# mLSTM cell and multiplicative FFN on one core: one pair of last products and its sums moved up two steps, y's transposes put ahead of k's and q's

## Chip, cores and metric

The kernel runs on one NeuronCore of one Trainium2 chip. The metric is the device time of one execution in microseconds (us); less is better. The engines are named as the profile names them: PE is TensorE (matmuls and transposes), PEld its weight loads, DVE is VectorE, ACT is ScalarE, POOL is GpSimd, SP is SyncE, which here only issues DMAs.

## The reference

Two blocks follow each other. The first is an mLSTM cell over 4 batches, 8 heads, 768 time steps and a head size of 40; the second is a feed-forward network on 3072 tokens of 320 features:

```python
for t in range(S):                       # 768 steps; q, k, v, gates are inputs
    m_new  = max(f_gate + m, i_gate)
    f_stab = exp(f_gate + m - m_new); i_stab = exp(i_gate - m_new)
    C = f_stab * C + i_stab * outer(v_t, k_t)
    n = f_stab * n + i_stab * k_t
    y_t = sigmoid(o_gate) * (C @ q_t) / max(abs(n . q_t), 1)
x = y as (3072, 320)
a = x @ w1; b = x @ w2                   # 320 x 1024 each
out = ((a * b) @ w3) @ w_out             # w3 1024 x 1024, w_out 1024 x 320
```

## The kernel before, in words

**Units and steps.** The tokens are cut into 24 units of 128 tokens of one batch (six stretches of time by four batches; `NU = 24`, `NT2 = 6`, `B = 4`). One Python loop over `s` writes 32 steps (0 to 31). In step `s` the cell forms the scores and the state of unit `s` and the outputs of unit `s-1` (`quarter_work`), and `y` of unit `s-2` is brought into the turned form `x` that the network needs. Everything is fp32. The program order of each engine is the order in which this loop writes its instructions; matmuls and transposes are chained by hand (`in_order`, used by `mm` at L92 and `transpose` at L95), so PE does exactly what is written, in that order.

**The first ten steps.** For units below 10, k and q are turned by PE: `turn(n)` writes four transposes of k and four of q into two PSUM tiles (`pt`), and ACT copies each out (`kT`, `qT`, L322). For units below 15, `y` is turned by PE too: `twice(n)` lets POOL copy 64 columns of `y` to its end (L467), `x_trans(n)` writes three transposes (`px`; the third one reads the copied columns) and one ACT copy into `xT` (L477). At the end of step `s`, `turn(s+1)` comes first and `x_trans(s-2)` after it. At these steps PSUM has four tiles for this work (`mps`, a ring of four). A matmul into a tile waits until the tile's last reader is done.

**The network.** Tokens go through in six groups of four units. For groups 0 to 2, `up` forms blocks of `a` and `b` (PSUM `pa`, `pb`; 128x256 moving), `up_rest` adds the last 64 of the 320 inputs, ACT scales `a` (`a_sb`, L626) and DVE multiplies into `ab` (L627). An `up` of half a group reads the `x` of two units: step 6 is the first to read units 2 and 3, step 8 the first to read units 4 and 5. w3 and w_out are multiplied together once (`wp`, then `w3o`), so that the last product is `ab @ w3o`; `ffn_out` does it for 14 blocks of 128 tokens.

**Seven products.** Groups 3 to 5 use a form with seven products of quarters for eight, at the price of sums. `up_by_seven` (one of 12 blocks in each of steps 19 to 30) is written in parts: `shared` (PSUM `p15`, `p67`, shown as `p`), `single` and `left` (PSUM `pa`, `pb`), `product`. DVE adds PSUM into the kept parts in `wo` (L674, L672), POOL finishes them (L699) and multiplies into `ab` (L717). `token_sums` are DVE's sums of `x` for it (L654, written to a tile named `w3T`), made after DVE has turned a late unit's `y` (`x_turn`, L463), which comes back from a trip through DRAM.

`out_by_seven` does the last product for five pairs of 128-token blocks: (3,1) in step 27, (4,0) in step 29 and three in step 31. Each has seven quarter products of PSUM tiles `o15`, `o67`, `o23`, `o4` (shown as `o`), an ACT copy (L777) and DVE sums (L782 to L785), and two DMAs out. It needs four sums of `ab` quarters (`ab_sums`, DVE, L758) and four of `w3o` quarters (`out_weight_sums`, POOL, L743: T1 to T4, made once). Before the change T1 is made in step 24, T2 and T3 in step 25, T4 in step 26, and the `ab` sums of pair (3,1) at the end of step 26, behind `x_turn` and `token_sums` in the program.

After step 24 the cell's PSUM is given back and `mps` is a ring of eight tiles. In step 27 the order on PE is: `shared` of the step's block, `out_by_seven(3,1)`, `single`, `left`.

Of the kernel before, what the change touches and what calls it, by code (L numbers as in the profile page):

```python
# [16 lines left out]
def kernel(  # L17
# [33 lines left out]
    NU = NT2 * B  # L51
# [42 lines left out]
    def transpose(out, in_, n=P):  # L94
        in_order(nc.tensor.transpose(out, in_, ident[0:n, 0:n]))  # L95
# [212 lines left out]
    def turn(n):  # L308


        if n >= N_DVE:
            for src, dst, name in zip(turned_in[n % 2], (kT_t, qT_t), ("kT", "qT")):
                dst[n] = sb.tile([128, NP, P], FP, name=name, tag=name)
                done = nc.vector.transpose(out=dst[n].rearrange("i p (r f) -> i p f r", f=4),
                                           in_=src[:, 32:TB].rearrange("i (p f d) -> i p f d", p=NP, f=4)[:, :, :, 0:32])
            return done
        for src, dst, name in ((kbuf[n % NB], kT_t, "kT"), (qbuf[n % NBQ], qT_t, "qT")):
            pt = mps([128, NP, P], "pt")
            for p in range(NP):
                transpose(pt[:, p, :], src[:, 2 * p:2 * p + 2, :].rearrange("p a b -> p (a b)"))  # L320
            dst[n] = sb.tile([128, NP, P], FP, name=name, tag=name)
            nc.scalar.copy(out=dst[n], in_=pt)  # L322
# [423 lines left out]
    wsums = out_weight_sums()  # L746
# [4 lines left out]
    def ab_sums(gr, j):  # L751
        mem = [t.rearrange("p h d -> p (h d)") if j == 0 else io.tile([P, H, L], FP, name="pw", tag="pw", bufs=5)
               .rearrange("p h t -> p (h t)") for t in kbuf]
        S1, S2, S3, S4 = S_o[gr, j] = [t.rearrange("p (f t) -> p f t", t=P) for t in mem]
        (A11, A12), (A21, A22) = quarters_of_ab(gr, j)
        for dst, p, q, op in ((S1, A21, A22, OP.add), (S2, S1, A11, OP.subtract), (S3, A11, A21, OP.subtract),
                              (S4, A12, S2, OP.subtract)):
            nc.vector.tensor_tensor(out=dst, in0=p, in1=q, op=op)  # L758
# [34 lines left out]
    outs = [(gr, j) for gr in range(3, NG) for j in range(2)][1:]  # L793
    summed = list(outs)
    sevens = [(gr, f) for gr in range(3, NG) for f in range(FH)]
    n_up = [0] * 2 + [1] * 4 + [2] * 10 + [0] * 16
    n_seven = [0] * 19 + [1] * 12 + [0]
    n_down = [0] * 16 + [2] * 5 + [1] * 4 + [0] * 7
    n_out = [0] * 27 + [1, 0, 1, 0, 3]
# [8 lines left out]
    for s in range(len(n_up)):  # L808
        if NY <= s - 2 < NU:
            send(s - 2)  # L810
        if N_U <= s + 3 < NU:
            load_u(s + 3)
        if s < 3:
            if s == 2:
                for _ in range(3):
                    fetch(*todo.pop(0))
            load(s + 2, slice(0, 2))
            if s == 1:
                load_o(2)
            if s == 2:  # L820
                for _ in range(2):
                    fetch(*todo.pop(0))
                fetched = 10
            load(s + 2, slice(2, 3))
            if s:
                load_o(s + 2)
        elif s + 2 < NU:
            load(s + 2)
            load_o(s + 2)
        if s < NU:  # L830
            if s >= B:
                decayed(state[s % B][1], state[s % B][0], s, 0)
        if 0 <= s - 2 < NY and s != 3:
            twice(s - 2)
        if NY <= s - 2 < NU:
            get_back(s - 2)
        while s >= N_DVE and turned < min(s - 2, NY):
            x_trans(turned)
            turned += 1
        fold()  # L840
        if s >= len(n_up) - 2:
            ab_sums(*summed.pop(0))
        seven = None
        if n_seven[s]:
            seven = up_by_seven(*sevens.pop(0), (lambda i: cell[i // 2][:, i % 2].rearrange("p (i t) -> p i t", i=2)) if s <= NU else
                                lambda i: mps([128, 2, TH], "p67" if i < 2 else "p15"), nc.gpsimd if sevens else nc.vector)
            if s <= NU:
                seven[0]()
            seven[1]()
        if seven and s <= NU:  # L850
            ffn_out([downs.pop(0) for _ in range(n_down[s])], [cell[1][:, i, 0:DM] for i in range(2)])
        else:
            for _ in range(n_down[s]):
                ffn_out([downs.pop(0)])
        for i in range(n_out[s]):
            out_by_seven(*outs.pop(0))
            if summed and n_out[s] > 1:
                ab_sums(*summed.pop(0))
        if seven and s > NU:
            seven[0]()  # L860
        now = [ups.pop(0) for _ in range(n_up[s])]
        open_ups = [up(*x) for x in now] if s != 2 else []
        if s == 3:
            turn(3)
        def rest():
            for x in open_ups:
                up_rest(*x)
            if seven:
                seven[2]()
            if s == 3:  # L870
                for _ in range(2):
                    convert()

        def between():
            twice(1)
            weighted(2)
            rows_of_u(3)
            for _ in range(3):
                scale_next()
            for n in range(2):  # L880
                x_trans(n)
                if n == 0:
                    warm(5)
            for _ in range(3):
                convert()
            turn(2)
            block = up(*now[0])
            weighted(3)
            weights(3)
            masks(3)  # L890
            out_gate(2)
            convert()
            up_rest(*block)

        gated = None
        if s <= NU:
            gated = quarter_work(s, rest, between if s == 2 else None)
        else:
            rest()
        with tc.issue_after(gated.ins) if gated else nullcontext():  # L900
            if seven:
                seven[3]()
            if NY <= s - 2 < NU:
                x_turn(s - 2)
            for n in () if s == 1 else (s + 2,) if s < B else (s + 2, s + 3) if s == B else (s + 3,):
                if n < N_U:
                    rows_of_u(n)
            if N_DVE <= s + 1 < NU:
                gated = turn(s + 1)
            if s - 2 in range(4 * GT - 1, NU, GT):  # L910
                token_sums((s - 2) // GT)
            for _ in range({NU: 1, NU + 1: 2, NU + 2: 1}.get(s, 0)):
                next(wsums)
            if s + 1 < len(n_up) - 1 and n_out[s + 1]:
                ab_sums(*summed.pop(0))
        if s == 0:
            weighted(1)
            weights(1)
            masks(1)
            gate_cols(g, gT, nc.scalar.copy)  # L920
        if s == NU:
            cell_psum.close()
            banks.extend([ps_m] * 3 + [ctx.enter_context(tc.tile_pool(name="ps_x", bufs=4, space=bass.MemoryType.PSUM))] * 4)
        if s in (2, 3):
            turned, converted = 2, converted + (4 if s == 2 else 2)
        if s + 1 < N_DVE:
            if s not in (1, 2):
                turn(s + 1)
            while turned < min(s - 1, NY):
                x_trans(turned)  # L930
                turned += 1
        if s < NU:
            if 0 < s < NU - 1 and s != 2:
                if s != 1:
                    weighted(s + 1)
                weights(s + 1)
                masks(s + 1)
            if s != 2:
                out_gate(s)
        if s in (16, 17):  # L940
            weight_sums(s - 16)
        if s == B:
            for i, r in enumerate(third):
                nc.sync.dma_start(out=U_d[i * GC:(i + 1) * GC].rearrange("c r t -> r c t"), in_=U3[r])
        with tc.issue_after(gated.ins) if N_DVE <= s + 1 < NU else nullcontext():
            for _ in range(n_cvt[s] if s < len(n_cvt) else 0):
                convert()
                converted += 1
        if s >= ahead:
            while pend and len(scaled) < 2:  # L950
                scale_next()
        if N_DVE <= s + 2 < NU:
            load_turned(s + 2)
        while todo and fetched < (n_fetch[s] if s < len(n_fetch) else converted + 4):
            fetch(*todo.pop(0))
            fetched += 1
        if s + 1 == pinned:
            for ins in keep_order(front):
                behind.enter_context(tc.issue_after(ins))
# [30 lines left out]
```

## Time and profile before

| what | value |
|---|---|
| median of three runs (lowest, highest) | 432.58 us (432.52, 433.48) |
| the profiled execution's own time | 433.62 us |
| its span, first to last instruction | 431.6 us |
| PE busy in the span | 415.4 us (96%) |
| DVE busy | 312.7 us (72%) |
| ACT, POOL busy | 149.5 us (35%), 154.7 us (36%) |
| mean granted TensorE clock | 0.992 |

A line of the profile's groups or of the timeline names an engine, the line of the kernel, the operation and the tiles as out<-in; a line of the waits names who waited, for whom, the sum, the number and the longest of the waits. The busy share of PE counts matmuls whose ends are modelled, so the stretches where PE has nothing to do at all are found in the waits and in the timeline, not in that share.

### The profile page before, as it was taken

The numbers are of one execution on the slowest core, as the hardware profiler recorded it, in microseconds if no ns is written. First come the engines' busy times: TensorE is split into PE (matmuls) and PEld (weight loads), VectorE is DVE, ScalarE is ACT, GpSimd is POOL, SyncE is SP. The second block draws the span as 40 slices with busy tenths as digits, with TensorE's granted clock in tenths as the row PEclk, the third lists the DMA queues.
The fourth block names the chain that finished last, engine by engine and source line by source line (L and its number), as shares of the span: only waits on it lengthen the run. The fifth ranks groups of instructions, "written<-read, shape, count | busy, mean of one in ns | idle before, by whom it ended". The sixth has DMA issues, their size and how long they took to land.

```text
span 431.6 us, 13076 instructions
## 1 busy us (share of the span) xinstructions
PE 415.4 (96%) x5353; PEld 340.8 (79%) x5353; DVE 312.7 (72%) x634; ACT 149.5 (35%) x404; POOL 154.7 (36%) x211
## 2 busy tenths in 40 slices
PE   7879989999999999999999999999999997999996
PEld 6778868878778788787777778688778777888896
DVE  5576986778949779778736966597866769575972
ACT  3857764566625524630332203033210111110000
POOL 4431342333303113203307752556444377342200
PEclk9969999999999999999999999999999999999999
DMA  8999978498887866885436665856321120000001
GB/s 185 217 170 226 224 118 149 111 194 169 213 173 149 183 180 132 180 168 112 83 83 132 157 127 128 150 122 123 73 56 26 29 38 0 32 2 30 2 32 61
DMA packets 135211, 51.15 MB, mean 119 GB/s; under 512 B 109360, under 2 KB 126960, under 8 KB 135152
## 3 DMA queue, kind: packets, MB, share of 16 engines
q1 hardware_dynamic: 131552, 46.29, 52.6%
q10 hardware_dynamic: 3600, 4.03, 2.7%
q8 instruction: 42, 0.69, 0.7%
q14 instruction: 17, 0.14, 0.1%
HBM read 44.50 MB, written 5.80 MB: 117 GB/s over the span
## 4 chain that ended last, share of the span: by engine, by line
PE 76%; issue 8%; DVE 5%; POOL 4%; DMA 4%; SPq 1%; ACT 1%; POOLq 0%; DVEq 0%; ACTq 0%
PE pa L92 20%; PE cell L92 19%; PE pb L92 13%; PE o L92 9%; PE wp L92 7%; PE p L92 3%; PE pt L95 2%; DVE w3T L654 1%; PE px L95 1%; POOL pw L305 1%; POOL raw L647 1%; DMA q_all<-in_q_dram 1%; DMA y_d<-y 1%; DMA pw<-U_d 1%; POOL state L332 1%
## 5 line engine op out<-in xcount | busy, mean ns | idle before, releaser
L332 POOL TENSOR_TENSOR state<-state,decay 128x164 f32<-128x164 f32 x40 | 19.3, 482 | 161.5 <-DVE state L397 122.1
L92 PE MATMUL pa<-xT,w 128*128 128x256 f32 x240 | 60.9, 384 | 2.4 <-ACT xT L477 1.6
L92 PEld LDWEIGHTS pa<-xT,w 128*128 128x128 f32 x240 | 44.6, 191 | 9.6 <-ACT xT L477 2.3
L300 ACT ACTIVATE pw<-pw,aT 128x64 f32<-128x64 f32 x184 | 46.4, 341 | 3.3 <-ACT o_sb L729 2.3
L92 PE MATMUL pb<-xT,w 128*128 128x256 f32 x192 | 45.4, 379 | 0.0
L717 POOL TENSOR_TENSOR ab<-ab,a_sb 128x512 f32<-128x512 f32 x22 | 29.1, 1343 | 36.1 <-DVE ab L672 36.1
L92 PEld LDWEIGHTS pb<-xT,w 128*128 128x128 f32 x192 | 36.5, 190 | 5.0
L305 POOL TENSOR_SCALAR_AFFINE_SELECT pw<-pw 64x512 f32<-64x512 f32 x48 | 37.4, 778 | 5.0 <-ACT pw L300 3.4
L699 POOL TENSOR_TENSOR wo<-wo 128x512 f32<-128x512 f32 x22 | 27.4, 1268 | 30.3 <-DVE wo L674 30.3
L92 PE MATMUL pa<-xT,wr 64*64 64x256 f32 x384 | 37.0, 386 | 0.0
L626 ACT ACTIVATE a_sb<-pa 128x512 f32<-128x512 f32 x24 | 14.3, 597 | 63.9 <-PE pb L92 63.9
L92 PE MATMUL pb<-xT,wr 64*64 64x256 f32 x384 | 36.4, 380 | 0.0
L92 PE MATMUL wp<-wo,w3T 128*128 128x320 f32 x128 | 35.8, 433 | 0.4 <-issue 0.4
L92 PE MATMUL cell<-w3o,ab 128*128 128x320 f32 x128 | 35.4, 432 | 0.0
L627 DVE TENSOR_TENSOR ab<-pb,a_sb 128x512 f32<-128x512 f32 x24 | 16.4, 688 | 25.3 <-ACT a_sb L626 25.2
L92 PEld LDWEIGHTS cell<-w3o,ab 128*128 128x128 f32 x128 | 24.3, 190 | 9.5
L92 PEld LDWEIGHTS wp<-wo,w3T 128*128 128x128 f32 x128 | 23.8, 190 | 9.6 <-issue 0.6
L92 PEld LDWEIGHTS pa<-xT,wr 64*64 64x64 f32 x384 | 18.9, 132 | 14.9 <-issue 9.1
L674 DVE SCALAR_TENSOR_TENSOR a_sb<-pa,wo 128x512 f32<-128x512 f32 x12 | 8.3, 689 | 30.1 <-PE pa L92 30.1
L421 DVE TENSOR_TENSOR h<-cell,h 64x164 f32<-64x164 f32 x88 | 28.7, 326 | 1.6
L92 PE MATMUL po<-w3o,ab 128*128 128x320 f32 x96 | 26.4, 433 | 0.0
L92 PEld LDWEIGHTS po<-w3o,ab 128*128 128x128 f32 x96 | 18.1, 190 | 7.3
(179 smaller groups left out, 850.6 us busy)
## 6 DMA issues: line engine op xcount, KB each, us to landing
raw<-in_moe_w_dram SPq DMA_DIRECT2D x64, 128.0 KB, 3.2
kbuf<-in_k_dram SPq DMA_DIRECT2D x24, 160.0 KB, 4.5
v_all<-in_v_dram SPq DMA_DIRECT2D x24, 160.0 KB, 4.8
o_in<-in_o_gate_dram SPq DMA_DIRECT2D x24, 160.0 KB, 4.6
pw<-U_d SPq DMA_DIRECT2D x28, 128.0 KB, 3.5
raw<-in_moe_w_dram SPq DMA_DIRECT2D x5, 512.0 KB, 6.2
raw<-in_moe_w_out_dram SPq DMA_DIRECT2D x8, 320.0 KB, 3.8
gates<-in_k_dram SPq DMA_DIRECT2D x28, 80.0 KB, 2.7
```

Of the source, the lines that this page charges most:

```text
L92: in_order(nc.tensor.matmul(out, lhsT=lhsT, rhs=rhs, start=start, stop=stop))
L95: in_order(nc.tensor.transpose(out, in_, ident[0:n, 0:n]))
L300: nc.scalar.activation(out=pw[:, h, :], in_=src[:, h, :], func=AF.Exp, bias=aT[:, c, b * H + h:b * H + h + 1])
L305: nc.gpsimd.affine_select(out=pw[r], in_=pw[r], compare_op=OP.is_ge, fill=0.0, base=0, pattern=[[0, H], [1, L]], channel_multiplier=-1)
L332: nc.gpsimd.tensor_tensor(out=new, in0=old, op=OP.mult, in1=decay[:, b * NP:(b + 1) * NP, 2 * c + x:2 * c + x + 1] .to_broadcast([P, NP, D1]))
L421: nc.vector.tensor_tensor(out=part, in0=ph[x][halves[e]], in1=part, op=OP.add)
L626: nc.scalar.mul(out=a_sb, in_=pa, mul=UP ** -2)
L627: nc.vector.tensor_tensor(out=ab_t[gr][j][:, fs[0]:fs[-1] + 1, t0:t0 + a_sb.shape[-1]], in0=pb, in1=a_sb, op=OP.mult)
L647: nc.gpsimd.tensor_tensor(out=dst, in0=p, in1=q, op=op)
L674: nc.vector.scalar_tensor_tensor(out=out, in0=p, scalar=UP ** -2, in1=q, op0=OP.mult, op1=OP.add)
L699: aside_by.tensor_tensor(out=kept[j][:, 1:4:2], in0=kept[j][:, 1:3], in1=kept[j][:, 3:4].to_broadcast([128, 2, TH]), op=OP.add)
L717: aside_by.tensor_tensor(out=t[:, f:FO:FH, :], in0=t[:, f:FO:FH, :], in1=a, op=OP.mult)
```

## The change

Three edits in the loop. First, in step 27 alone, the pair's `out_by_seven` is written ahead of the step's `up_by_seven` block, where it stood between the block's `shared` and `single`. Second, the sums for that pair move up: the four `ab` sums from the end of step 26 to step 25, ahead of `x_turn` and `token_sums` of that step; T4 from step 26 to step 25 behind T2 and T3. The sums for the later pairs stay where they were. Third, at the end of each step below nine `x_trans` is written ahead of `turn(s+1)`; there are five steps in which both occur (4 to 8).

```diff
         if s >= len(n_up) - 2:
             ab_sums(*summed.pop(0))
+        def pairs():
+            for i in range(n_out[s]):
+                out_by_seven(*outs.pop(0))
+                if summed and n_out[s] > 1:
+                    ab_sums(*summed.pop(0))
+
         seven = None
+        if s == NU + 3:
+            pairs()
         if n_seven[s]:
             seven = up_by_seven(...)
...
-        for i in range(n_out[s]):
-            out_by_seven(*outs.pop(0))
-            if summed and n_out[s] > 1:
-                ab_sums(*summed.pop(0))
+        if s != NU + 3:
+            pairs()
         if seven and s > NU:
             seven[0]()
...
             if seven:
                 seven[3]()
+            for _ in range({NU: 1, NU + 1: 3}.get(s, 0)):
+                next(wsums)
+            if s == NU + 1:
+                ab_sums(*summed.pop(0))
             if NY <= s - 2 < NU:
                 x_turn(s - 2)
...
-            for _ in range({NU: 1, NU + 1: 2, NU + 2: 1}.get(s, 0)):
-                next(wsums)
-            if s + 1 < len(n_up) - 1 and n_out[s + 1]:
+            if s < len(n_up) - 2 and n_out[s + 1] and s > NU + 2:
                 ab_sums(*summed.pop(0))
...
         if s + 1 < N_DVE:
-            if s not in (1, 2):
-                turn(s + 1)
             while turned < min(s - 1, NY):
                 x_trans(turned)
                 turned += 1
+            if s not in (1, 2):
+                turn(s + 1)
```

The counts are the same before and after on every engine. In the built program PE, ACT, DVE and POOL differ in the places named and nowhere else; SP's order is the same.

## The prediction

> **What bounds the kernel now.** I read the page first. Its first part has PE busy nearly the whole span:
>
> ```profile
> PE 415.4 (96%) x5353; PEld 340.8 (79%) x5353; DVE 312.7 (72%) x634; ACT 149.5 (35%) x404; POOL 154.7 (36%) x211
> ```
>
> The chain of waits agrees: from 246 us to the end it is almost wholly PE, but for one stretch at 338 to 364 us. So the time is PE's work plus the moments in which PE has nothing to do, and an edit that leaves the work alone is worth the moments that it removes, less those that it makes. The list of PE's waits has the ones near the change:
>
> ```profile
> PE pa L92 <- ACT xT L477: 1.6, 2, 0.8
> ...
> PE o L92 <- DVE pw L758: 1.4, 1, 1.4
> ...
> PE pa L92 <- DVE den L429: 0.8, 1, 0.8
> PE o L92 <- issue: 0.5, 1, 0.5
> ...
> PE o L92 <- PE o L92: 0.4, 1, 0.4
> ...
> PE px L95 <- POOL y L467: 0.2, 1, 0.2
> ```
>
> Two are early (network blocks waiting for ACT's copy of the turned y), three are in the first pair's products. What the pair costs I read by cutting windows at the first matmul of `shared` in steps 27, 28 and 29. The columns are window, length, then busy time of PE, PEld, DVE, ACT, POOL, granted clock, DMA share:
>
> ```profile
> 25.00:28.40 3.40, 3.23 (x29) 3.15 (x30) 2.17 (x7) 0.57 (x2) 0.00 (x0) 0.50 1.10 170
> 28.40:31.70 3.30, 3.27 (x15) 2.92 (x14) 3.16 (x5) 1.24 (x3) 2.07 (x3) 0.50 1.02 227
> ...
> 354.43:373.24 18.81, 16.45 (x120) 14.05 (x116) 15.19 (x25) 1.61 (x3) 9.88 (x7) 1.00 0.05 18
> 373.24:381.37 8.13, 8.13 (x64) 6.36 (x60) 4.25 (x9) 1.18 (x2) 4.95 (x4) 1.00 0.00 0
> ```
>
> Step 27 takes 18.81, the plain step 28 takes 8.13. The pair of step 29, whose sums are early, is one row of the chain, `PE o` x56, 7.61 us from 385.09. So step 27 should take 8.13 + 7.61 = 15.74, and 3.07 us of it are loss: the three waits (2.3) and what PE loses around each[...]. (The first two rows are for the slow rival.)
>
> [...] DVE's pair sums run beside POOL's L717 and L743, and the last one runs alone:
>
> ```profile
> 358.71 2.94 POOL L717 TENSOR_TENSOR ab<-ab,a_sb 128x512 f32<-128x512 f32 x2 [0.17 <-DVE ab L672]
> 359.18 1.34 DVE L758 TENSOR_TENSOR pw<-ab 128x512 f32<-128x512 f32 x1
> 360.56 1.64 DVE L758 TENSOR_TENSOR pw<-pw,ab 128x512 f32<-128x512 f32 x1
> 361.62 1.99 POOL L743 TENSOR_TENSOR q_all<-w3o,gates 128x640 f32<-128x640 f32 x1
> 362.12 2.02 DVE L758 TENSOR_TENSOR pw<-ab 128x512 f32<-128x512 f32 x1
> 364.07 0.68 DVE L758 TENSOR_TENSOR pw<-ab,pw 128x512 f32<-128x512 f32 x1
> ```
>
> A sum takes 0.68 alone and 1.34 to 2.02 beside POOL; each ends about 0.5 after the POOL instruction it met. [...] Here it was 0.50 from 25.0 to 31.7, after idle times of 1.2 and 2.2 close together; single ones of 1.2 and 1.4 later did nothing.
>
> **Part 1: y's transposes first, steps 4 to 8.** Work is unchanged; three transposes pass eight, and on ACT `xT` passes `kT` and `qT`. Only where the next step reads the new `xT` can it pay: step 6 (units 2 and 3) and step 8 (units 4 and 5). Around step 5's end:
>
> ```profile
> 60.74 0.66 PE L95 MATMUL pt<-ident,kbuf 128*128 128x128 f32 x4
> ...
> 61.67 0.49 PE L95 MATMUL px<-ident,y 128*128 128x128 f32 x3
> 61.97 0.59 ACT L322 COPY qT<-pt 128x512 f32<-128x512 f32 x1
> 62.45 0.50 ACT L477 COPY xT<-px 128x384 f32<-128x384 f32 x1
> ```
>
> With `px` at 60.74 its copy runs from about 61.4 to 61.9, while PE does the eight others until 62.0. In step 7, where nothing waits, `pa` starts 0.16 before `px` ends (74.96, 75.12). So `pa` could start at 62.16 - 0.16 = 62.00 for 63.00: **1.00 gained**. Step 8 likewise: 87.76 - 86.82 = **0.94 gained**. `kT` and `qT` come 0.5 later on ACT, first read some 10 us later by the score products: nothing. The exponentials behind the three copies start when they did.
>
> Step 4 loses. The third `px` needs POOL's L467, and that is late:
>
> ```profile
> 50.70 0.82 DVE L436 TENSOR_TENSOR y<-h,o_in 128x320 f32<-128x320 f32 x1
> 51.32 0.66 PE L95 MATMUL pt<-ident,kbuf 128*128 128x128 f32 x4
> ...
> 52.53 0.24 POOL L467 COPY y<-y 128x64 f32<-128x64 f32 x1
> ...
> 52.82 0.33 PE L95 MATMUL px<-ident,y 128*128 128x128 f32 x1 [0.19 <-POOL y L467]
> ```
>
> Now eight transposes fill PE from 51.32 on, and 0.19 is left to wait. With `px` in front PE stands until 52.82, and the eight (one per 0.108: 0.86) come after it: **0.86 lost**. Queued behind it are `kT` and `qT`, so the exponentials end 1.3 later, near 56.9, and POOL's masks (56.81) start 0.3 later; unit 3's L467 moves from 59.07 to 59.4, still ahead of its `px` after 60.74. In steps 5 to 8 L467 ends more than a microsecond ahead of `px` (59.30 against 60.74; 67.64 against 73.70). Steps 4, 6 and 8 gain nothing by the order. The 0.8 at 100.64 named DVE has no reader of that copy; I leave it at nothing (between 0 and 0.9 gained, because it ends 0.03 after the copy does).
>
> Sum of part 1: 1.00 + 0.94 - 0.86 = **1.1 gained**. PE has no wait over 0.1 from 148 to 245 us, so it should carry to there; the 0.4 at 245 (`pa` on DVE's L654) ends a chain DVE-DMA-DVE that starts from PE's step 18 and moves with it.
>
> **Part 2: sums at step 25.** DVE is idle for 4.01 before L463 (348.76 to 352.77, waiting for y's DMA), where four sums alone would fit (2.6). But POOL is at L717 and L743 from 348.20 to 353.69, and T4 adds 1.54. At one sum for each POOL instruction I place the sums at 348.76, 350.1, 351.7, 353.7 and their end near 355.5; T4's near 356.6. L463 then slips by 2.8, L654 ends near 358.3 (was 355.1), L674 near 359.2 (was 355.9), `ab` near 362.9 (was 359.3). Nobody waits for T4's place in POOL's queue: the L699 behind it waits for L674 anyway.
>
> **Part 3: the pair first in step 27.** It starts at 354.43. S1, T1, S2, T2, S3, T3 are needed from 355.5 to 357.7 and are there by 355.0. PSUM tiles: `o15` and `o67` take tiles that ACT has freed by 349.5. `o23`, due at 358.8, takes the one that L674 frees at 359.2: **0.45 lost** (between 0 and, if POOL shuts DVE out altogether, 3.2). `o4`, due 361.0, `p` due 362 and 364, `pa` due 366 need DVE results of about 360.0, 361.6, 362.9 and 364: 1 us or more to spare. The token sums, due at 354.4 before, are due at 362. The rest of the step's DVE sums come behind and are done by 367.4, before `left` ends.
>
> So step 27: 3.07 - 0.45 = **2.6 gained**. After it PE stays the bound to the end (no PE wait in the list after 364), and all moves together.
>
> **Sum.** 1.1 + 2.6 = 3.7. The profiled execution took 433.62 (span 431.6 and 2.0 around it): 429.9. The median, 432.58, lies 1.0 below that execution, so 428.9. Measurements of this kernel can tell about 0.3% (1.3 us) from no change.
>
> **Rivals.**
> *All of it, no conflict* (17%). The sums find DVE free between POOL's instructions, and the wait at 100.64 goes with the copy: 3.07 + 1.94 + 0.9 - 0.86 = 5.05 gained, 427.5. Against: the durations of L758 above.
> *The early gain is absorbed* (15%). DVE is 90% busy around 48 to 60, DMA 80 to 100% busy until 130; if the loads and not PE's steps set the pace on the way to 245, only step 27 pays: 2.6, 430.0. Against: PE waits for nothing from 148 to 245.
> *POOL shuts DVE out* (12%). The sums begin when POOL pauses at 356.6; L674 frees its tile at 362.0, PE stands 3.2 in the pair, part 3 gives nothing: 1.1, 431.5. A new wait for the one removed. Against: in 359 to 364 one sum passed per POOL instruction.
> *PE's clock falls* (3%), the slow case. The new wait in step 4 (1.4, from 51.4) is followed at 59.2 by 1.2 of issue; together they might halve the clock as at 25 us. [...]
> That the change does not do what it says is excluded: the built program's order shows each move.
>
> **How the numbers follow.** The likeliest case (53%) is 428.9, its own range 428.0 to 429.9. The range 427.3 to 430.9 takes in the first two rivals, and leaves out most of the last two, about 15% with tails. Faster by over 0.3% (below 431.3): 53 + 17 + 15 and a fifth of the third rival, less some for what I have not seen: 0.87. Within 0.3%: 0.10. Slower: 0.03.
>
> **What would show it.** After: `pa` of steps 6 and 8 with no wait for L477; a wait of `px` for L467 of about 1.2 (or 1.4 with that for y) in step 4; L758 of pair (3,1) near 347 to 354 with durations over 1; step 27 from `o` to the next step's `shared` 15.7 to 16.2; at most 0.5 of wait in the `o` group, named DVE wo L674. I am wrong if step 27 is over 17, if `px` in step 4 doesn't wait, or if PE gets a wait of over 1 us between 100 and 340.

## The result and the profile after

The changed kernel takes **429.28 us** (median of four runs, 428.33 to 429.91) against 432.59 (432.52 to 433.48): ratio 0.9917, 95% interval 0.9893 to 0.9940, so 3.3 us gained where 3.7 were forecast. The profiled execution took 428.33, its span 426.3 (before: 433.62 and 431.6). The profiled execution is the quickest of the four, so the two spans differ by more than the medians; the sizes below are taken stage by stage.

The first part of the page says that PE's work is unchanged in number and that PE is still busy nearly all the time:

```profile
PE 411.2 (96%) x5353; PEld 337.2 (79%) x5353; DVE 312.5 (73%) x634; ACT 149.7 (35%) x404; POOL 156.6 (37%) x211
```

The list of PE's waits (who waited, for whom, the sum, the number, the longest):

```profile
PE cell L92 <- issue: 3.0, 2, 2.7
...
PE px L95 <- POOL y L467: 0.7, 1, 0.7
PE px L95 <- DVE y L436: 0.5, 1, 0.5
...
PE wp L92 <- DVE ab L627: 0.4, 1, 0.4
...
PE o L92 <- DVE wo L674: 0.2, 1, 0.2
```

The two waits for ACT's `xT` (L477) and the one for L758 are gone. In their place stand those of `px` in step 4 (0.5 for `y`, 0.7 for POOL's copy), a small one of `wp`, and 0.2 in the pair. Steps 27 and 28 by windows, now cut at the pair's first product and at the next steps' `shared` (window, length, then busy time of PE, PEld, DVE, ACT, POOL, granted clock, DMA share):

```profile
351.75:367.95 16.20, 15.99 (x120) 13.99 (x116) 11.97 (x24) 1.50 (x3) 10.35 (x8) 1.00 0.06 21
367.95:376.08 8.13, 8.13 (x64) 6.37 (x60) 4.26 (x9) 1.18 (x2) 4.94 (x4) 1.00 0.00 0
```

Step 27 went from 18.81 to 16.20: **2.61 gained**, and PE is busy for all but 0.21 of it. The timeline shows where the sums went:

```profile
345.52 2.94 POOL L717 TENSOR_TENSOR ab<-ab,a_sb 128x512 f32<-128x512 f32 x2 [0.17 <-DVE ab L672]
345.99 1.34 DVE L758 TENSOR_TENSOR pw<-ab 128x512 f32<-128x512 f32 x1
...
347.37 1.64 DVE L758 TENSOR_TENSOR pw<-pw,ab 128x512 f32<-128x512 f32 x1
...
348.42 1.98 POOL L743 TENSOR_TENSOR gates<-w3o,v_all 128x640 f32<-128x640 f32 x1
...
348.93 2.02 DVE L758 TENSOR_TENSOR pw<-ab 128x512 f32<-128x512 f32 x1
...
350.88 2.02 DVE L758 TENSOR_TENSOR pw<-ab,pw 128x512 f32<-128x512 f32 x1
...
352.83 0.56 DVE L463 STREAM_TRANSPOSE xT<-yb 128x384 f32<-128x384 f32 x1
```

Each sum meets a POOL instruction and takes 1.34 to 2.02, one per POOL instruction, as before the change; only now PE has other work meanwhile. At the early end the timeline of step 4 shows the new wait, and that of step 5 the copy of `xT` done under the eight other transposes:

```profile
50.40 0.82 DVE L436 TENSOR_TENSOR y<-h,o_in 128x320 f32<-128x320 f32 x1
...
51.36 0.41 PE L95 MATMUL px<-ident,y 128*128 128x128 f32 x2 [0.53 <-DVE y L436]
52.23 0.23 POOL L467 COPY y<-y 128x64 f32<-128x64 f32 x1
...
52.52 0.33 PE L95 MATMUL px<-ident,y 128*128 128x128 f32 x1 [0.74 <-POOL y L467]
...
60.42 0.48 ACT L477 COPY xT<-px 128x384 f32<-128x384 f32 x1 [1.52 <-PE px L95]
...
60.66 0.60 PE L95 MATMUL pt<-ident,q_all 128*128 128x128 f32 x4
...
61.09 1.24 PE L92 MATMUL pa<-xT,w 128*128 128x256 f32 x5
```

The copy ends at 60.90, and `pa` follows the transposes at 61.09 without a wait.

### The profile page after: what moved, and what is told of

Same layout as the page of the kernel before. It is cut to its first block, busy times and chain, and to the rows that moved or that the text cites. A ratio compares the mean times of both kernels' runs of the same rounds, so it can differ in the third digit from the quotient of the medians.

```text
span 426.3 us, 13079 instructions
## 1 busy us (share of the span) xinstructions
PE 411.2 (96%) x5353; PEld 337.2 (79%) x5353; DVE 312.5 (73%) x634; ACT 149.7 (35%) x404; POOL 156.6 (37%) x211
## 4 chain that ended last, share of the span: by engine, by line
PE 72%; issue 11%; DVE 5%; POOL 5%; DMA 4%; SPq 1%; ACT 0%; DVEq 0%; POOLq 0%
PE pa L92 19%; PE cell L92 19%; PE pb L92 12%; PE o L92 8%; PE wp L92 6%; PE p L92 3%; POOL pw L305 2%; DVE w3T L654 1%; PE pt L95 1%; PE px L95 1%; POOL raw L647 1%; DMA v_all<-in_v_dram 1%; DMA y_d<-y 1%; POOL state L332 1%; DMA pw<-U_d 1%
## 5 line engine op out<-in xcount | busy, mean ns | idle before, releaser
L92 PE MATMUL pa<-xT,w 128*128 128x256 f32 x240 | 60.5, 383 | 0.0
L92 PEld LDWEIGHTS pa<-xT,w 128*128 128x128 f32 x240 | 44.4, 190 | 6.7 <-ACT xT L477 0.5
L92 PE MATMUL pb<-xT,w 128*128 128x256 f32 x192 | 45.4, 379 | 0.0
L92 PEld LDWEIGHTS pb<-xT,w 128*128 128x128 f32 x192 | 36.5, 190 | 4.9
L92 PE MATMUL pa<-xT,wr 64*64 64x256 f32 x384 | 37.0, 386 | 0.0
L92 PE MATMUL wp<-wo,w3T 128*128 128x320 f32 x128 | 36.0, 434 | 0.9 <-issue 0.5
L92 PE MATMUL pb<-xT,wr 64*64 64x256 f32 x384 | 36.4, 380 | 0.0
L92 PE MATMUL cell<-w3o,ab 128*128 128x320 f32 x128 | 35.4, 432 | 0.0
L627 DVE TENSOR_TENSOR ab<-pb,a_sb 128x512 f32<-128x512 f32 x24 | 16.4, 687 | 23.0 <-ACT a_sb L626 22.8
L92 PEld LDWEIGHTS wp<-wo,w3T 128*128 128x128 f32 x128 | 23.7, 190 | 10.5 <-issue 1.0
L92 PEld LDWEIGHTS cell<-w3o,ab 128*128 128x128 f32 x128 | 24.3, 190 | 9.5
L92 PEld LDWEIGHTS pa<-xT,wr 64*64 64x64 f32 x384 | 18.9, 132 | 14.8 <-issue 9.1
L674 DVE SCALAR_TENSOR_TENSOR a_sb<-pa,wo 128x512 f32<-128x512 f32 x12 | 8.3, 688 | 29.9 <-PE pa L92 29.9
L421 DVE TENSOR_TENSOR h<-cell,h 64x164 f32<-64x164 f32 x88 | 28.7, 326 | 1.7
L92 PE MATMUL po<-w3o,ab 128*128 128x320 f32 x96 | 26.4, 434 | 0.0
L92 PEld LDWEIGHTS po<-w3o,ab 128*128 128x128 f32 x96 | 18.1, 190 | 7.3
```

The source lines that it names most:

```text
L92: in_order(nc.tensor.matmul(out, lhsT=lhsT, rhs=rhs, start=start, stop=stop))
L421: nc.vector.tensor_tensor(out=part, in0=ph[x][halves[e]], in1=part, op=OP.add)
L627: nc.vector.tensor_tensor(out=ab_t[gr][j][:, fs[0]:fs[-1] + 1, t0:t0 + a_sb.shape[-1]], in0=pb, in1=a_sb, op=OP.mult)
L674: nc.vector.scalar_tensor_tensor(out=out, in0=p, scalar=UP ** -2, in1=q, op0=OP.mult, op1=OP.add)
```

## The experiments

Single executions of one kernel lie up to 5 us apart (431.04 to 436.07 in one set of 27 of the kernel before). The traces show much of such a spread early: step 4 starts anywhere from 47.1 to 49.5 us in them, while from step 10 to the end those with the same late part agree within 0.8. So two measures are used: the ratio to the kernel before, timed beside it, and the lengths of stages in the traces (one execution of each kernel), from the first product (`cell<-v_all,pw`) of one step to that of the next. "Old" is `turn` first, "new" `x_trans` first; the last column is how long PE stands, by a wait named issue, behind its 976th matmul, which is in step 5:

| kernel | order in step 4 | in 5, 7 | 4 to 5 | 5 to 6 | 7 to 8 | 8 to 10 | stop at matmul 976 |
|---|---|---|---|---|---|---|---|
| before | old | old | 7.95 | 14.43 | 12.90 | 32.49 | 1.22 |
| e2_late | old | old | 8.57 | 14.43 | 12.90 | 32.48 | 1.22 |
| e3_pair_first | old | old | 8.58 | 14.43 | 12.91 | 32.47 | 1.22 |
| e4_sums_early | old | old | 8.57 | 14.70 | 12.91 | 32.47 | 1.49 |
| e6_not4 | old | new | 8.58 | 13.32 | 11.86 | 33.18 | 1.22 |
| e10_t3 | old | new | 8.57 | 13.05 | 11.86 | 32.47 | 0.94 |
| e5_5and7 | old | new | 9.59 | 11.85 | 11.85 | 32.48 | none |
| e7_only4 | new | old | 9.45 | 12.96 | 12.91 | 32.49 | none |
| e8_only4_dve | new, copy on DVE | old | 8.89 | 14.43 | 12.90 | 32.48 | 1.22 |
| e11_after_dve | new, copy on DVE | new | 8.27 | 13.33 | 11.86 | 32.92 | 1.22 |
| after | new | new | 9.45 | 11.86 | 11.86 | 32.61 | none |
| e0_after (after again) | new | new | 11.11 | 11.85 | 11.86 | 32.43 | none |
| e1_early | new | new | 11.43 | 11.86 | 11.86 | 32.44 | none |

In e0, e1 and e5 the granted clock was at half for part of the stage 4 to 5, see below. In e6 and e11 PE stops for issue once more between 8 and 10 (0.77 and 0.51). The stage 6 to 7 is 11.85 or 11.86 in all thirteen.

**The early part alone (e1_early)** and **the late part alone (e2_late)**.

```diff
 e1: the kernel before, with x_trans ahead of turn(s + 1)
 e2: the changed kernel, with turn(s + 1) ahead of x_trans
```

> Only y's transposes first (steps 3 to 9), step 27 as in the kernel before. Theory (two gains, one loss, carried to step 27): 1.1 us faster, 431.5; steps 6 and 8 start their cell without a wait for ACT L477, px in step 4 waits for POOL L467, step 27 keeps its 18.8. Rival A (the early gain is absorbed before step 27): 432.6, no change. Rival B (all of the 1.75 that the trace of after shows between steps 4 and 12 belongs to the order): 430.8.

> Only the sums two steps sooner and the pair first in step 27; the transposes in the old order. Theory: 2.6 us faster, 430.0; step 27 takes 16.2 (18.8 before), with a wait of 0.2 to 0.5 for DVE L674 as the only one. Rival (the whole 3.3 of after comes from here and the early part gives nothing): 429.3, step 27 at 15.5.

Measured: e1 431.92 against 432.63, ratio 0.9980 (0.9956 to 1.0004, 14 runs); e2 429.68, ratio 0.9931 (0.9905 to 0.9957). In us, e1 gains 0.9 (from -0.2 to 1.9) and e2 3.0 (1.9 to 4.1); together 3.9, where the whole change by its ratios (0.9917 in the first runs, 0.9907 in e0_after) gains 3.6 and 4.0. The parts add up within what can be told. By windows e2's step 27 is as in the changed kernel, and e1's is the old one, 18.81. Here is e2's:

```profile
352.67:368.89 16.22, 16.00 (x121) 14.00 (x117) 12.01 (x24) 1.50 (x3) 10.36 (x8) 1.00 0.06 21
```

The late part is settled: step 27 is 2.6 us shorter, and the timed gain, 3.0, agrees. The early part by itself is not told from nothing by its time; the rest of the experiments on it work with the stages.

**Halves of the late part: e4_sums_early (sums early, pair behind `shared`) and e3_pair_first (pair first, sums late).**

```diff
 e4: e2_late with
-        if s == NU + 3:
-            pairs()
...
-        if s != NU + 3:
-            pairs()
+        pairs()
 e3: e2_late with the sums' lines as in the kernel before
```

> As e2_late, but the pair stays behind the shared block of step 27: the sums alone are moved. Theory (the sums push L463 and the token sums L654 back by 2.8, and shared reads them first): p waits about 2.4 for L654 where it waited for nothing, the pair then waits for nothing, so step 27 takes about 18.1 to 18.4 and the time is 0.3 to 0.7 below before, near 432.1. Rival (early sums are all that counts, the order within step 27 doesn't matter): 430.0 as e2_late or a little less, 429.5.

> The pair first in step 27, its sums where they were (end of step 26), transposes in the old order. Theory (the sums of the pair end at 364.7 whatever PE does, so the pair ends no earlier and the shared block of 3.4 comes after it instead of under the wait): PE waits some 5 for L758 in the pair, step 27 lasts about 22.1, time 436.0. Rival (the order in step 27 alone gives the gain): 430.0.

Measured: e4 432.93, ratio 1.0007 (0.9989 to 1.0025); e3 437.15, ratio 1.0118 (1.0093 to 1.0142), 5.1 slower (4.0 to 6.2). Neither half gains; only both do. PE's waits in step 27 are the ones named, e3's first:

```profile
PE o L92 <- DVE pw L758: 4.9, 1, 4.9
```

```profile
PE p L92 <- DVE w3T L654: 2.2, 1, 2.2
```

In e4 the four sums hold DVE's queue, L463 and L654 come behind them, and `shared` needs L654 at once. But both steps are longer than the forecast's 15.74 of work and the wait: 19.72 for 17.9 in e4, 22.55 for 20.6 in e3. The windows name the rest. Here are e4's, cut around its wait:

```profile
353.36:356.76 3.40, 1.21 (x7) 0.79 (x4) 3.33 (x5) 0.00 (x0) 2.55 (x2) 0.88 0.00 0
356.76:360.16 3.40, 3.40 (x11) 2.71 (x10) 3.27 (x8) 0.00 (x0) 1.90 (x2) 0.62 0.00 0
360.16:363.56 3.40, 3.40 (x25) 3.30 (x24) 2.85 (x7) 1.47 (x3) 3.23 (x4) 1.00 0.00 0
```

After 2.2 of waiting PE's clock is at half for (0.12 + 0.38) x 3.40 / 0.5 = 3.4 us. PE has no wait in that stretch, so this costs about 1.7: 19.72 - 1.7 = 18.0. In e3 the mean clock of step 27 is 0.92, which is (1 - 0.92) x 22.55 = 1.8, about the same loss. In the kernel before, 1.8 of waiting in the same place (1.4 and 0.4) left the clock at 1.00.

**Step 4: e5_5and7, e6_not4, e7_only4**, and the changed kernel again (e0_after). In these the new order is used in some steps only.

```diff
+            if s in (5, 7):          # e5; e6: s > 4; e7 (from the kernel before): s == 4
+                while turned < min(s - 1, NY):
+                    x_trans(turned)
+                    turned += 1
             if s not in (1, 2):
                 turn(s + 1)
```

> The change, but y's transposes go first only in steps 5 and 7; in steps 4, 6 and 8 the old order. Theory (step 4 lost 1.5 in the trace of after and steps 4, 6, 8 gain nothing by the order): 1.5 below after if nothing takes its place, 427.8; 0.9 by the forecast's price, 428.4. Rival (PE's wait in step 4 let something be done that otherwise stops PE at 59.2 for 1.2, named issue in the trace of before): that stop comes back and the time is only 0.3 below after, 429.0.

> The changed kernel again, beside the next ones. 429.3 +- 0.5. Theory: in step 4 px waits 0.7 to 1.2 (DVE L436, POOL L467), PE does not stop for issue at its 976th matmul (in step 5), and from the start of step 5 to that of step 10 it takes 68.2 (71.7 to 71.9 with the old order).

> The change, but step 4 keeps the old order (steps 5 to 8 the new one). Theory (forecast's price of step 4): 0.9 below after, 428.4; step 4 lasts 8.0 to 8.6. Rival (PE's wait in step 4 costs little, because without it PE runs into the stop for issue at its 976th matmul, 1.2 to 1.5): that stop is there, and the time is within 0.4 of after.

> The kernel before with the new order in step 4 alone. Theory (forecast's price): 0.9 above before, 433.5; step 4 lasts 0.9 to 1.5 longer, 8.8 to 9.5, and the waits for ACT L477 in steps 5 and 7 stay. Rival (the wait in step 4 takes the place of the stop for issue at PE's 976th matmul): that stop is gone and the time is that of before, within 0.3.

Measured: e5 429.03, ratio 0.9915 (0.9886 to 0.9944); e0 428.86, 0.9907 (0.9877 to 0.9938); e6 429.29, 0.9913 (0.9885 to 0.9940); e7 434.31, **1.0024** (1.0007 to 1.0042, 22 runs). The times of e5 and e6 are not told from the changed kernel's, and with intervals of 1.2 us to either side they could not tell 0.9 from nothing. So the table has to answer, in pieces:

- The wait for `xT` in step 6 is worth 12.96 - 11.86 = 1.10 (e7 against after, neither with a stop), or 14.43 - 13.32 = 1.11 (e2 against e6, both with one); that at step 8, 12.90 - 11.86 = 1.04.
- The order in step 4 costs 9.45 - 8.58 = 0.87 in the stage 4 to 5 (e7 against e6).
- From 8 to 10 it is 32.43 to 32.61 in eleven of the thirteen, whatever the order, and the other two have an added stop. The wait of 0.8 at 100.64, named `den` L429 in before, does not belong to the old order: e2 and e3 have that order and not this wait. They wait 0.6 and 0.7 for `ab` L627 near 110 us instead, as e0 (0.7) does with the new order. With or without it the stage takes the same (32.49 in before, 32.48 in e2).
- Where the stage 4 to 5 takes 8.9 or less, PE stops for 0.9 to 1.5 in step 5; where it takes 9.45 or more, for whatever reason, it doesn't. So on PE the wait in step 4 (0.87) takes away a stop that is a little larger than itself (1.22). In e5 step 4 kept the old order and was long by its half clock, so e5 decides nothing between its two lines. The counts in the windows from 0 to that stop show that it is one place of the program: kernel before, then e6, then e8.

```profile
0.00:59.20 59.20, 53.08 (x976) 46.02 (x976) 42.24 (x100) 37.96 (x104) 21.55 (x57) 0.94 0.96 196
```

```profile
0.00:59.10 59.10, 47.94 (x976) 40.59 (x976) 41.92 (x101) 38.01 (x104) 22.72 (x57) 0.97 0.96 196
```

```profile
0.00:59.20 59.20, 50.11 (x976) 42.76 (x976) 42.13 (x102) 38.06 (x104) 22.20 (x56) 0.91 0.95 196
```

PE has done exactly 976 matmuls and 976 weight loads each time. So by the stages undoing step 4 should give nothing. But e7 is 1.0 slower than before (0.3 to 1.8), which its stages don't show (4 to 10: 79.66, before 79.63). Its trace is of its quickest execution of 22 (431.18, median 434.31), so what the others lose need not be in it. The expectation's rival was right that the stop goes and wrong about the time.

**The wait in step 4 made smaller: e8_only4_dve.**

```diff
-        nc.gpsimd.tensor_copy(out=y_t[n][:, DM:DM + REM], in_=...)
+        (nc.vector if n == 2 else nc.gpsimd).tensor_copy(out=y_t[n][:, DM:DM + REM], in_=...)
```

> e7_only4 with unit 2's copy of L467 on DVE, right behind y, so that px of step 4 waits for y alone. Theory (e7 is 1.2 slower than before because PE stands 1.2 in step 4, 0.74 of it for POOL's L467): the wait for L467 is gone, that for y (0.5) stays, step 4 lasts about 8.7 instead of 9.45, and the time lies 0.7 below e7, 433.6. Rival (the clock, not the wait itself, is what e7 pays with: its runs' mean granted clock is 0.985, that of the kernel before 0.989): the clock is back at 0.988 or more and the time within 0.3 of before, 432.6 to 433.2.

Measured: 433.12 against 433.80 beside it, ratio 0.9991 (0.9974 to 1.0008, 22 runs). The stage 4 to 5 is 0.56 shorter than in e7, since DVE's copy still lets `px` wait 0.2, and the stop at matmul 976 is back. By the ratios e8 is 0.33% or 1.4 us better than e7, give or take 1.0, although its stop is back; so the stages of these traces may not tell all of e7's loss. The mean granted clock of the runs goes the same way: 0.9850 in e7 (0.9885 in the kernel before beside it), 0.9861 in e8 (before 0.9873), and 0.9854 in e1 (before 0.9898). A difference of 0.0035 is 1.5 us of full clock in 430. How it can look is seen in e0 and e5, windows of 3.4 over stage 4 to 5; e0 (order new) first:

```profile
49.50:52.90 3.40, 3.04 (x109) 2.56 (x101) 3.12 (x6) 0.00 (x0) 3.20 (x6) 0.50 0.98 328
52.90:56.30 3.40, 3.39 (x13) 3.12 (x14) 2.82 (x11) 2.18 (x6) 0.51 (x2) 0.50 0.99 168
56.30:59.70 3.40, 3.40 (x26) 2.66 (x28) 3.23 (x7) 2.53 (x9) 2.44 (x5) 0.99 0.48 83
```

```profile
49.50:52.90 3.40, 3.39 (x76) 3.35 (x77) 3.32 (x7) 1.05 (x2) 2.50 (x5) 0.66 1.12 333
52.90:56.30 3.40, 3.40 (x15) 2.90 (x15) 2.87 (x10) 3.40 (x13) 1.23 (x3) 0.84 0.95 139
```

In both the clock falls behind waits that end with step 3 (the last one, 1.5, ends at 48.97 in e0 and 48.25 in e5), ahead of `px`: the order in step 4 doesn't start it. With the new order it lasted 6.8 us, with the old one 3.4. Three traces of this kind (e0 and e1 new, e5 old) fit a longer fall with the wait in step 4, and don't prove it.

**Does the stop belong to a place in PE's program? e9_shift.**

```diff
                 if n == 0:
                     warm(5)
+                    small = mps([P, P], "fill")
+                    for _ in range(24):
+                        mm(small[0:64, 0:16], ident[0:64, 0:64], ident[0:64, 0:16])
```

> The kernel before with 24 small matmuls (64x64 by 64x16) more at the place of warm(5), so that every later instruction of PE stands 48 places further on. Theory (the stop for issue in step 5 belongs to a place in PE's instruction stream[...]): the stop comes again after 976 matmuls, now 24 matmuls earlier in the work. Rival (it belongs to the work there): it comes after 1000 matmuls. No stop at all would leave this open. Time within 1 of before.

Measured: 446.21 in one run, far off: the trace counts 48 small matmuls and 48 weight loads for the 24 lines, they took 5.2 us, and the clock was at half around them (0.50 from 24.4 to 38.0 us). The stops are what it was run for. They come behind these counts, the first one ahead of the added matmuls:

```profile
0.00:22.80 22.80, 19.36 (x345) 16.78 (x345) 13.21 (x39) 14.75 (x48) 9.73 (x37) 1.00 0.98 197
```

```profile
0.00:56.80 56.80, 51.30 (x850) 45.13 (x851) 34.80 (x83) 32.60 (x89) 16.40 (x48) 0.88 0.97 197
```

```profile
0.00:82.90 82.90, 74.08 (x1229) 64.43 (x1230) 52.13 (x124) 44.37 (x122) 24.86 (x63) 0.88 0.85 165
```

Not at 976 and not at 1024, so neither line of the expectation holds as written: 850 less the 48 is matmul 802 of the other kernels, where none of them stops. But the places are regular. The windows count matmuls and weight loads; the trace also records PE's semaphore instructions (13 of them up to matmul 218, 33 up to 976). With all three counted, PE's stops in the table below all lie behind instruction 193 + 256 x n of PE, in e9 as in the other kernels. These places are numbered by n:

| n | PE instructions ahead | matmuls ahead | traces that stop there | length of the stop | from the landing of packet n to PE's next matmul |
|---|---|---|---|---|---|
| 1 | 449 | 218 | after, e10 | 0.24, 0.67 | 1.08, 1.54 |
| 2 | 705 | 345 | all but e10 | 0.37 to 2.73 | 1.28 to 1.69 |
| 6 | 1729 | 850 | e9 | 2.49 | 1.40 |
| 7 | 1985 | 976 | the eight of the table | 0.94 to 1.49 | 1.27 to 1.48 |
| 9 | 2497 | 1229 | e9 | 1.72 | 1.30 |
| 12 | 3265 | 1607 or 1609 | before, e4, e6, e7, e8, e11 | 0.22 to 0.77 | 1.33 to 1.67 |
| 17 | 4545 | 2244 or 2245 | before, after, e0, e1, e4 to e7 | 0.16 to 0.66 | 1.37 to 1.55 |
| 19 | 5057 | 2500 | e9 | 0.32 | 1.42 |

The changed kernel's page has a DMA queue of the kind `instruction` with 42 packets, and the 2 x 5353 matmuls and weight loads of PE are 41.8 times 256:

```profile
q8 instruction: 42, 0.69, 0.8%
```

The trace has the time of each packet, and the last column of the table sets it beside the stop. The stop at place n ends 1.1 to 1.7 us after the n-th packet has landed, in all forty cases, and of all such places in the fourteen traces none is passed sooner than 1.08 after its packet. In the kernel before packet 7 is on its way from 57.63 to 59.00, PE stands from 59.24, and goes on at 60.46. In the five traces without the stop at matmul 976 the packet had landed 2.4 to 4.9 before PE came there; in e9 it had landed 7.4 before.

So the stop belongs to a place in PE's program, as the theory had it, and comes when the packet of that place lands late; the 96 instructions more in e9 put other work there. The stops took 0.2 to 2.7 us. What a packet holds, and what sets the moment at which it comes, is not shown.

The names of waits can mislead here, since they are inferred. The waits named `den` L429 (before at 100.64, and e7) and `h` L421 (e4, e8) lie exactly on place 12 and end 1.33 to 1.67 after packet 12, so they are most likely stops of this kind too. On the other hand the stop named issue near 47 us behind matmul 690 (1.5 in nine of the traces, 0.9 in e4) lies on no such place. It ends 0.10 after DVE's L390 in all ten, which writes the `pw` that the stopped products read: that is a wait for data.

**Two attempts at a better kernel: e10_t3 (T2 and T3 a step sooner, order as e5) and e11_after_dve (the change with e8's copy).**

```diff
-            for _ in range({NU: 1, NU + 1: 3}.get(s, 0)):     # e10
+            for _ in range({NU: 3, NU + 1: 1}.get(s, 0)):
```

> As e5_5and7, with T2 and T3 (POOL L743) in step 24 behind T1, T4 alone in step 25. Theory (a sum of L758 takes 1.3 to 2.0 only beside a POOL instruction): in step 25 two sums meet L717 and one meets T4, the fourth takes 0.68 alone; the sums end at about 1.3 less behind their start than in after (5.6 for 6.9), L463 and L674 come 1.3 sooner, and the wait of 0.2 in the pair goes: step 27 lasts 16.0. Time 0.2 below e5_5and7, which is not to be told from it. Rival (DVE's sums are slow there for another reason): the fourth sum takes 2.0 again and step 27 16.2.

> The whole change, with unit 2's copy of L467 on DVE as in e8_only4_dve: the version that the runs point to. Theory (step 4's wait costs 1.0 to 1.4 in e7 against e8, clock included): about 1 below after, 428.0, mean granted clock 0.99. Rival (with a shorter step 4 PE meets the stop for issue at its 976th matmul again, 1.2, which eats it): the stop is there and the time is that of after, 429.0.

Measured: e10 428.31, ratio 0.9875 (0.9840 to 0.9911); e11 429.47, 0.9918 (0.9887 to 0.9948). Both beat the kernel before, neither is told from the changed one. In e10 the fourth sum did take 0.68 alone, but step 27 got longer, 16.53, with a wait of 0.5 for L674. The timeline shows why:

```profile
339.90 1.54 POOL L743 TENSOR_TENSOR gates<-w3o,v_all 128x640 f32<-128x640 f32 x1
341.39 1.79 POOL L743 TENSOR_TENSOR gates<-w3o 128x640 f32<-128x640 f32 x1
```

```profile
340.12 1.66 DVE L434 SCALAR_TENSOR_TENSOR o_in<-o_in,den 128x320 f32<-128x320 f32 x1
341.82 1.72 DVE L436 TENSOR_TENSOR y<-h,o_in 128x320 f32<-128x320 f32 x1
...
351.03 2.02 DVE L758 TENSOR_TENSOR pw<-ab 128x512 f32<-128x512 f32 x1
352.98 0.68 DVE L758 TENSOR_TENSOR pw<-ab,pw 128x512 f32<-128x512 f32 x1
```

L434 and L436 took 0.49 each in the changed kernel; beside the moved T2 and T3 they take 1.66 and 1.72, all that follows on DVE is 2.1 later, and the sums end 0.8 later than before the move. The slow instructions beside POOL were moved, not removed. In e11 the rival held: the stop at matmul 976 is back, 1.22 (table of the stages), and the time is not told from that of the changed kernel.

## Why the prediction was right, and where it was off

**The result** (429.28) is 0.4 from 428.9 and inside the likeliest case's own range.

**Part 2, the sums.** Right in mechanism, order and time. By step 25 the changed kernel is 2.7 ahead of the kernel before, so 348.76, 350.1, 351.7, 353.7 become 346.1, 347.4, 349.0, 351.0; measured 345.99, 347.37, 348.93, 350.88. L463 comes at 352.83 (forecast in the same way 352.9).

**Part 3, the pair.** Forecast 2.62, measured 2.61. The wait for L674's tile is 0.20 for 0.45, and yet the step gained no more, because PE is busy for 15.99 of it where the forecast had 15.74 of work and put nothing around that wait. The two differences cancel, so an agreement to 0.01 is in part luck. e3 and e4 show that the two edits need each other: the sums alone are paid for by `shared` waiting for the token sums, the order alone waits 4.9 for the sums.

**Part 1, the transposes.** The three terms are right: 1.10 for 1.00, 1.04 for 0.94, 0.87 for 0.86. Against before's own trace step 4 lost 1.50. Of the 0.62 more, 0.25 is a `px` that waited only 0.19 there and 0.44 in five other kernels with the old order; another 0.33 lies ahead of the changed place, where `cell<-qT,kT` comes 0.80 behind the products before it in after, e2 and e6, and 0.47 in before. The wait at 100.64 was rightly put at nothing: 8 to 10 takes the same without it.

What failed is a term that the sum left out. The list of waits before had "PE cell L92 <- issue: 3.4, 2, 2.2", of which 1.2 lay in the stage that the change shortens. I used it only as fuel for a falling clock and took it as fixed. This stop ended 1.27 to 1.48 after packet 7 of the `instruction` queue in the eight traces that have it, and is missing in the five in which that packet had landed 2.4 to 4.9 before PE came there. So the wait in step 4 costs less on PE than 0.87, and with the old order in step 4 (e6) the stop is there again. That makes PE's stages from 4 to 10 gain 2.0 in the trace of after (79.63 to 77.63), and 2.6 against e2 (80.24), the late part alone. They gain only 0.2 and 0.5 in e1 and e0, whose clock fell there. Timed, the early part gave 0.9 (-0.2 to 1.9). The forecast of 1.1 lies between these, and that is partly luck: a stop of 1.2 that it did not count went, and falls of the clock that it did not count took some of that back.

**The rivals.** "No conflict" fell with the durations of L758. "Absorbed" fell by the traces: the gain of the early part is still there at step 25 (2.68 ahead in the two traces, 0.9 of it from before step 4, where nothing was changed). By the times alone it would stand, since the interval of e1 takes in no gain. "POOL shuts DVE out" fell: one sum passed per POOL instruction. "PE's clock falls" was put at 3%; a fall as long as that from 25.0 to 31.7 in the kernel before (6.7 us at a granted clock of 0.50) would have cost, as an estimate, half its length, 3.4 of the 3.7. As a cause of a slower kernel it did not come; but a fall in the stage 4 to 5 is in three traces (e0, e1, e5), begun after waits in step 3, and the loss of e7 (1.0, with a lower mean clock) may come from it. That is left open.

## What to carry to other kernels

When a consumer is moved ahead, move what feeds it in the same edit, and ask who stands behind the moved producer in its queue: here sums alone gained nothing, order alone lost 5 us, and both gained 2.6. Before taking a sum's duration from the profile, look at what POOL does in the same microseconds at the new place: a sum of L758 took 0.68 alone and 1.34 to 2.02 beside POOL, and in e10 the moved T2 and T3 put L434 and L436 from 0.49 to 1.66 and 1.72. A wait named "issue" need not be a property of the work there: with 96 instructions more ahead (e9) PE stopped behind matmul 850 and not behind 976. Count the instructions ahead of such a wait and compare it with the packets of the instruction queue; if they fit, as here, where PE went on 1.1 to 1.7 after the landing, price an edit ahead of it by when the packet lands and when the engine arrives, not by adding its wait to the sum.

## What the runs showed of the hardware

- PE stopped for 0.2 to 2.7 us at places a multiple of 256 of its instructions apart (matmuls, weight loads and semaphore instructions counted), and went on 1.1 to 1.7 us after the packet of the same number in the queue of the kind `instruction` had landed, forty times in fourteen traces. With 48 matmuls and their loads put ahead (e9) the stops lay in the same series of counts (705, 1729, 2497, 5057) and, behind the added matmuls, met other work.
- A wait of 2.2 in one piece (e4) or 4.9 (e3) was followed by one stretch of 3.4 us at half clock, about 1.7 us lost beyond the wait; waits of 1.4 and 0.4 within 3 us (the kernel before) were not. PE was not idle for all of the time ahead of a fall: over the last 3.4 us it was busy for 1.5 in e4 (352.5 to 356.0) and for 1.7 in e9 (55.1 to 58.5). Stretches of the same length with as little work, 1.72 in the kernel before (359.4 to 362.8), 1.56 in e8 and 1.30 in e10 (both 45.2 to 48.6), were not followed by one. No threshold comes out of these traces.
- DVE's L434 and L436 (128x320) went from 0.49 to 1.66 and 1.72 us beside POOL's 128x640 subtraction (e10), which itself took 1.54 to 1.79 (1.98 beside L758). A small instruction met it too: L431 (128x8) took 1.46 beside the subtraction at 338.59 of the changed kernel, and 0.16 in step 3.
